# Linformer attention and maxout FFN on one core: softmax sums of a batch in one bank by 128x32 column tiles, spread over partitions by DMA

## The chip, the cores and the metric

The kernel runs on one core of a Trainium2 chip. The metric is device time in microseconds (us). A measured time is some 2 us longer than the span that the profile of the same execution shows (405.52 us against 403.5 us before), so spans are compared with spans and times with times. PE is TensorE, PEld its weight loads, DVE is VectorE, ACT is ScalarE, POOL is GpSimd, SP is SyncE; SPq is SP's sequencer, which here only issues DMAs.

## The reference, cut to what matters

```python
k_proj = einsum('ks,bhsd->bhkd', E, k)            # 1024 keys become 64; v with F likewise
scores = scale * matmul(q, k_proj^T)               # 8 batches, 8 heads, 1024 queries, 64 keys
attn   = exp(scores - max) / (sum(exp) + 1e-9)
x      = matmul(attn, v_proj) -> [8192, 512]       # heads side by side
h      = max(x @ w1, x @ w2, x @ w3)               # 512 -> 768, three times
out    = h @ w_out                                 # 768 -> 512
```

## The kernel before

The FFN runs batch by batch, in two chunks of 512 tokens. A chunk is six `up` steps of 12 matmuls (128x512) and four `down` groups of 6. The attention of batch n is woven into the FFN of batch n-1: a plan says which pieces are put behind which step. The key `(ch, step)` is chunk and step; steps 0 to 5 are `up`, 6 to 9 are `down`. So batch 3's attention stands in the plan of b = 2.

Scores are kept with keys on partitions, so that the sum over keys is a matmul with ones. It gives every sum 64 times, on the very partitions where it is needed:

```python
def pair_mm(b, g, lo, nsi, w):              # one pair of heads: four 64x64 matmuls, side by side
    t, ns = two()                           # two PSUM banks of eight
    p = pTs[b, g, lo]                       # exp(scores)
    for c in range(2):
        rows = slice(c * HALF, (c + 1) * HALF)
        for hp in range(2):
            nc.tensor.matmul(out=t[hp * HALF:(hp + 1) * HALF, c, 0:nsi * HALF],
                             lhsT=w(rows, hp), rhs=p[rows, hp, :], start=True, stop=True)
    ...
def za(b, g, ...):                          # sums, values, inversion, multiply of one pair
    z  = sums(b, g, lo, nsi)                # pair_mm with ones
    av = values(b, g, lo, nsi)              # pair_mm with v_proj
    invert(b, g, lo, nsi, z)                # ACT: Ln, then Exp(-x), each 128x1024
    scale_x(b, g, lo, nsi, av)              # DVE: xT = av * zi, 128x1024
def qd(b):                                  # turn the queries of batch b
    ...                                     # four DVE copies into q_p
    last_T[b] = nc.sync.dma_start_transpose(out=qTs[b]..., in_=q_p...)     # SP's queue
# plan, b == 2                                    # plan, b >= 3 (n = b + 1)
(0, 2): [kproj(3), vproj(3), ld(4)],              (0, 1): [za(n, 0), sc(n, 1)],
(0, 3): [kt(3)],                                  (0, 3): [za(n, 1), sc(n, 2)],
(0, 4): [sc(3, 0)],                               (0, 6): [qd(n + 1)],
(0, 6): [za(3, 0), sc(3, 1)],                     (0, 9): [za(n, 2), sc(n, 3),
(1, 0): [za(3, 1), sc(3, 2), qd(4)],                       kproj(n + 1), vproj(n + 1)],
(1, 2): [za(3, 2), sc(3, 3), kproj(4), ...],      (1, 1): [kt(n + 1), ld(n + 2)],
(1, 4): [kt(4)], (1, 5): [za(3, 3), sc(4, 0)]     (1, 3): [za(n, 3), sc(n + 1, 0)]
```

The transposes, the stores of the output and, after the change, the new DMAs all go through SP, which issues them in the order of the program, each with its wait (the profile after shows a store that was ready at 144.09 us leave at 151.71, behind a transpose).

Names in the profiles: `q_p` and `qT` are the queries before and after the transpose, `pT` is exp(scores), `vp` the projected values, `xT` the attention's output that the up matmuls read, `h1s` a copy of the first up product, `m` and `hT` the two maxima (the down matmuls read `hT`), `zd` and `zi_all` the inverted sums in DRAM and on the partitions. `banks` is PSUM, the eight banks that matmuls write.

The softmax here doesn't subtract the row's maximum and nothing guards it: scores larger than these inputs give would overflow.

## Time and profile before

The median of three runs is 405.52 us (405.26 to 405.64).

| what | where it is read | value |
|---|---|---|
| PE busy | page, part 1 | 98% of a 403.5 us span |
| PE busy in the FFN of batches 3, 4, 5 | stretches | 47.18 of 47.25, 47.00 of 47.00, 47.00 of 47.00 us |
| sums and values of a pair; scores of a pair | chain of waits | 0.56 us; 0.22 us |
| DVE, ACT busy in such a stretch | stretches | 23.94 us each |

The busy time of each engine in stretches that I cut where a batch's last down group ends in the chain (columns: stretch, its length, PE, PEld, DVE, ACT, POOL busy with instruction counts, granted clock as a share of full speed, DMA share, GB/s; the DMA share adds up the packets' times over 16 engines and can pass 1). Here those of the FFN of batches 2 to 5 of the kernel before:

```profile
122.47:172.70 50.23, 49.91 (x313) 23.24 (x312) 25.51 (x40) 25.48 (x37) 5.26 (x6) 1.00 0.93 179
172.70:219.95 47.25, 47.18 (x276) 21.20 (x274) 23.94 (x36) 23.94 (x34) 2.63 (x3) 1.00 0.87 176
219.95:266.95 47.00, 47.00 (x276) 21.22 (x274) 23.94 (x36) 23.94 (x34) 2.63 (x3) 1.00 0.67 134
266.95:313.95 47.00, 47.00 (x275) 21.30 (x274) 23.94 (x36) 23.94 (x34) 0.00 (x0) 1.00 0.22 69
```

PE has no gap there to win back: only work taken off PE can shorten a stretch. The chain of waits (start, length, what) shows what that work costs. L222 is `pair_mm`, L202 the scores, L508 the up matmuls:

```profile
219.95 5.18 PE banks L508 x24
225.13 0.56 PE banks L222 x8
225.69 0.22 PE banks L202 x4
225.91 5.29 PE banks L508 x24
```

Twenty-four up matmuls take 5.18 us, 0.216 us each, and 5.29 after attention work: I put the 0.11 us down to the return to the 128x128 shape. Four 64x64 matmuls side by side take about 0.22 us, and going to that shape takes about 0.12 us more (0.56 - 2 x 0.22).

### The profile page before, as it was taken

How to read it: one execution, taken by the hardware profiler on the slowest of the kernel's cores; microseconds unless marked ns; L12 is line 12 of the kernel's file. 1: busy time of each engine (PE TensorE's matmuls, PEld its weight loads, DVE VectorE, ACT ScalarE, POOL GpSimd, SP SyncE). 2: the span in 40 equal slices, each digit the busy share in tenths (PEclk: the TensorE clock that was granted, in tenths of full speed). 3: DMA queues.
4: the chain of work that ended last, by engine and by line, in shares of the span. 5: the costliest groups of instructions: out<-in, count | busy, mean ns of one | idle time of the engine just before them, and what ended most of it. 6: DMA issues, size and time to landing. Idle time of an engine off the chain costs nothing.

```text
span 403.5 us, 5873 instructions
## 1 busy us (share of the span) xinstructions
PE 394.5 (98%) x2351; PEld 178.5 (44%) x2351; DVE 203.5 (50%) x314; ACT 189.4 (47%) x274; POOL 31.6 (8%) x44
## 2 busy tenths in 40 slices
PE   7899999999999999999999999999999999999996
PEld 3444444344444435444544445444544444444443
DVE  2348755761764527537353655626364363525251
ACT  2622537525672376555643555437535555432322
POOL 7340001001000100200100002000000000000000
PEclk9999999999999999999999999999999999999999
DMA  8999999959907996992799029960510202020202
GB/s 150 207 205 207 231 201 163 246 119 193 219 2 215 190 222 106 137 241 40 210 180 208 30 15 238 201 173 0 137 73 2 104 2 104 0 106 0 106 0 105
DMA packets 62667, 53.33 MB, mean 132 GB/s; under 512 B 30128, under 2 KB 58288, under 8 KB 62640
## 3 DMA queue, kind: packets, MB, share of 16 engines
q0 software_dynamic: 28512, 28.31, 44.1%
q1 hardware_dynamic: 33984, 24.51, 20.6%
q8 instruction: 18, 0.29, 0.3%
q10 hardware_dynamic: 144, 0.13, 0.1%
q14 instruction: 9, 0.07, 0.1%
HBM read 57.15 MB, written 16.78 MB: 183 GB/s over the span
## 4 chain that ended last, share of the span: by engine, by line
PE 82%; DMA 11%; ACT 2%; DVE 1%; POOL 1%; issue 1%; DVEq 0%; ACTq 0%; POOLq 0%
PE banks L508 56%; PE banks L605 18%; DMA v_t<-in_v_dram 7%; PE banks L222 4%; DMA w_sb<-in_moe_w_dram 3%; PE banks L286 3%; PE banks L202 2%; ACT zi L241 1%; DVE xT L252 1%; ACT zl L235 1%; DMA out_dram<-o_sb 0%; POOL k_t L148 0%; POOL q_t L153 0%; POOL v_t L148 0%; DVE m L570 0%
## 5 line engine op out<-in xcount | busy, mean ns | idle before, releaser
L508 PE MATMUL banks<-xT,w_sb 128*128 128x512 bf16 x1152 | 257.9, 379 | 1.5 <-DMA w_sb<-in_moe_w_dram 1.2
L508 PEld LDWEIGHTS <-w_sb 128*128 128x128 bf16 x1152 | 109.5, 98 | 138.1 <-issue 10.6
L570 DVE TENSOR_TENSOR m<-banks,h1s 128x512 f32<-128x512 f32 x90 | 62.1, 690 | 85.0 <-ACT h1s L566 52.1
L566 ACT COPY h1s<-banks 128x512 f32<-128x512 f32 x90 | 52.5, 583 | 90.3 <-PE banks L508 88.2
L605 PE MATMUL banks<-wout_sb,hT 128*128 128x512 bf16 x378 | 85.7, 379 | 0.1
L252 DVE TENSOR_TENSOR xT<-banks,zi 128x1024 bf16<-128x1024 f32 (+1 forms) x36 | 39.8, 1106 | 73.6 <-ACT zi L241 54.2
L518 DVE TENSOR_TENSOR hT<-banks,m 128x512 bf16<-128x512 f32 x90 | 62.3, 692 | 10.0 <-PE banks L508 0.8
L99 ACT COPY o_sb<-banks 128x512 f32<-128x512 f32 (+1 forms) x56 | 32.6, 581 | 52.4 <-PE banks L605 52.4
L605 PEld LDWEIGHTS <-hT 128*128 128x128 bf16 x378 | 36.0, 98 | 45.5 <-issue 3.1
L235 ACT ACTIVATE zl<-banks 128x1024 f32<-128x1024 f32 (+1 forms) x36 | 33.5, 930 | 31.4 <-PE banks L222 30.5
L213 ACT ACTIVATE pT<-banks 128x1024 bf16<-128x1024 f32 (+1 forms) x36 | 33.2, 930 | 15.5 <-PE banks L202 15.5
L241 ACT ACTIVATE zi<-zl 128x1024 f32<-128x1024 f32 (+1 forms) x36 | 34.6, 962 | 1.2
L191 POOL DMA_DIRECT2D q_t<-in_q_dram x7 | 6.2, 880 | 202.4 <-DVE kp L99 80.2
L222 PE MATMUL banks<-pT,ones 64*64 64x512 bf16 (+1 forms) x144 | 13.7, 374 | 0.7 <-DVE xT L252 0.3
L222 PE MATMUL banks<-pT,vp 64*64 64x512 bf16 (+1 forms) x144 | 13.3, 355 | 0.4 <-DVE vp L99 0.4
L202 PE MATMUL banks<-qT,kpT 64*64 64x512 bf16 (+1 forms) x144 | 13.3, 358 | 0.3 <-DVE m L570 0.3
L286 PEld LDWEIGHTS <-efT 128*64 128x64 bf16 x224 | 11.6, 110 | 3.4 <-issue 2.7
L99 DVE CAST vp<-banks 64x256 bf16<-64x256 f32 (+1 forms) x18 | 7.1, 397 | 7.6 <-ACT vp L99 3.7
L222 PEld LDWEIGHTS <-ones 64*64 64x64 bf16 x144 | 4.4, 103 | 14.3 <-issue 14.2
L99 DVE COPY q_p<-q_t 128x1024 bf16<-128x1024 bf16 x28 | 10.0, 420 | 0.0
L99 ACT CAST vp<-banks 64x256 bf16<-64x256 f32 x14 | 5.1, 365 | 8.9 <-PE banks L286 8.7
L99 DVE COPY o_sb<-banks 128x512 f32<-128x512 f32 (+1 forms) x9 | 5.8, 654 | 4.5 <-DMA out_dram<-o_sb 4.5
(51 smaller groups left out, 106.5 us busy)
## 6 DMA issues: line engine op xcount, KB each, us to landing
out_dram<-o_sb SPq DMA_DIRECT2D x30, 512.0 KB, 3.2
q_t<-in_q_dram POOLq DMA_DIRECT2D x7, 1024.0 KB, 9.4
k_t<-in_k_dram POOLq DMA_DIRECT2D x7, 1024.0 KB, 13.6
v_t<-in_v_dram POOLq DMA_DIRECT2D x7, 1024.0 KB, 18.6
w_sb<-in_moe_w_dram POOLq DMA_DIRECT2D x5, 384.0 KB, 12.7
k_t<-in_k_dram POOLq DMA_DIRECT2D x2, 512.0 KB, 8.9
v_t<-in_v_dram POOLq DMA_DIRECT2D x4, 256.0 KB, 12.2
wout_sb<-in_moe_w_out_dram POOLq DMA_DIRECT2D x1, 768.0 KB, 15.7
```

Of the source, the lines that this page charges most:

```text
L99: done = {"v": nc.vector.tensor_copy, "s": nc.scalar.copy, "g": nc.gpsimd.tensor_copy}[eng](out=o, in_=i)
L213: nc.scalar.activation(out=pTs[b, g, lo], in_=t, func=AF.Exp, scale=scale)
L222: nc.tensor.matmul(out=t[hp * HALF:(hp + 1) * HALF, c, 0:nsi * HALF], lhsT=w(rows, hp), rhs=p[rows, hp, :], start=True, stop=True,)
L235: nc.scalar.activation(out=zl, in_=t, func=AF.Ln)
L241: nc.scalar.activation(out=zi, in_=zl, func=AF.Exp, scale=-1.0)
L252: nc.vector.tensor_tensor(out=xTs[b][:, g, lo:lo + nsi, :].rearrange("a (c s) p -> a c (s p)", c=2), in0=t, in1=zi, op=ALU.mult,)
L286: nc.tensor.matmul(out=t[hh * HALF:(hh + 1) * HALF, 0:width], lhsT=efT[:, si, (kv - 1) * KP:kv * KP], rhs=qkv[b][kv][:, heads[hh], si, :], ...
L508: nc.tensor.matmul(out=h, lhsT=w_sb[i][:, ct, jt * P:(jt + 1) * P], rhs=xTs[b][:, ct, ch * SPC:(ch + 1) * SPC, :], start=(ct == first), st ...
L518: nc.vector.tensor_tensor(out=o, in0=h, in1=other, op=ALU.max)
L566: nc.scalar.copy(out=h1s, in_=h[0][0])
L570: nc.vector.tensor_tensor(out=m12, in0=h[1][0], in1=h1s, op=ALU.max)
L605: nc.tensor.matmul(out=o_ps, lhsT=hTs[b, ch][:, jt, tt * P:(tt + 1) * P], rhs=wout_sb[:, jt, :], start=(jt == 0), stop=(jt == NJT - 1),)
```

## The change

The intent: every sum is needed 64 times, but it need be computed only once. `pick` holds, for each head of a pair and each half of the chunk, a block of ones in 8 columns. All 16 rows of sums of a batch come from eight matmuls of 128x32 into one bank; ACT inverts one 128x512 tile instead of four of 128x1024; a small store (32 KB) and four broadcasts (512 KB each) through DRAM put the inverses on the 128 partitions. To give the DMAs time, scores and sums move to the start of the first chunk, and values with their multiplies (`vx`) to the second chunk.

```diff
+            for hp in range(2):
+                for g in range(NPAIR):
+                    nc.tensor.matmul(
+                        out=t[32 * g:32 * (g + 1), :], lhsT=pick[:, hp, :],
+                        rhs=pTs[b, g, 0][:, hp, :], start=(hp == 0), stop=(hp == 1),
+                    )
+            nc.scalar.activation(out=zlc, in_=t, func=AF.Ln)
+            nc.scalar.activation(out=zic, in_=zlc, func=AF.Exp, scale=-1.0)
+            nc.sync.dma_start(out=zd.rearrange("g h c f -> (g h c) f"),
+                              in_=zic.rearrange("(a r) f -> a r f", r=8)[:, 0, :])
+            for u in range(2):
+                gs = slice(2 * u, 2 * u + 2)
+                for hp in range(2):
+                    nc.sync.dma_start(out=zi_all(b)[hp * HALF:(hp + 1) * HALF, gs],
+                                      in_=zd[gs, hp].partition_broadcast(HALF))
 ...  plan, b == 2
+                (0, 0): [kproj(3), vproj(3), ld(4)],
+                (0, 1): [kt(3)],
+                (0, 2): [sc(3, 0, now=True), sc(3, 1)],
+                (0, 4): [sc(3, 2, now=True), sc(3, 3)],
+                (0, 5): [qd(4)],
+                (0, 6): [zc(3)],
+                (1, 2): [kproj(4), vproj(4), ld(5), vx(3, 0), vx(3, 1)],
+                (1, 3): [kt(4)],
+                (1, 5): [vx(3, 2), vx(3, 3), sc(4, 0)],
 ...  plan, b >= 3
+            (0, 1): [sc(n, 1, now=True), sc(n, 2, now=True), sc(n, 3)],
+            (0, 3): [zc(n)],
+            (1, 2): [vx(n, 0), vx(n, 1)],
+            (1, 4): [vx(n, 2), vx(n, 3)],
+            out[0, 2] = [qd(n + 1)]
+            out[1, 2] = [kproj(n + 1), vproj(n + 1)] + out[1, 2]
+            out[1, 3] = [kt(n + 1)]
+            out[1, 4] += [sc(n + 1, 0)]
```

(Cut: the plan's lines that these replace, the loads' places, the tiles, `vx`, six instead of four buffers for exp(scores), one buffer for the inverses of a whole batch.)

More of the change, by code (lines that the diff above doesn't have):

```diff
@@ L52 @@
     att = ctx.enter_context(tc.tile_pool(name="att", bufs=2))
+    scratch = ctx.enter_context(
+        tc.tile_pool(name="scratch", bufs=2, space=bass.MemoryType.DRAM)
+    )
     psum = ctx.enter_context(tc.tile_pool(name="psum", bufs=1, space=bass.MemoryType.PSUM))
@@ L119 @@
     ones = const.tile([P, HALF], BF16, name="ones")
+    pick = const.tile([P, 2, 32], BF16, name="pick")
     warm = const.tile([P, 512], BF16, name="warm")
@@ L174 @@
     nc.vector.memset(ones, 1.0)
+    nc.vector.memset(pick, 0.0)
+    for hp in range(2):
+        for c in range(2):
+            at = hp * 16 + c * 8
+            nc.vector.memset(pick[c * HALF:(c + 1) * HALF, hp, at:at + 8], 1.0)
     load_w(0, slice(0, 2))
@@ L211, in exps @@
         t, ns, ready = sc
-        pTs[b, g, lo] = att.tile([P, 2, CHUNK], BF16, name="pT", bufs=4)[:, :, 0:nsi * HALF]
+        pTs[b, g, lo] = att.tile([P, 2, CHUNK], BF16, name="pT", bufs=6)[:, :, 0:nsi * HALF]
         nc.scalar.activation(out=pTs[b, g, lo], in_=t, func=AF.Exp, scale=scale)
@@ L230, in sums, with zi_all, zc, f @@
         return pair_mm(b, g, lo, nsi, lambda rows, hp: ones[rows])
+    zi_alls = {}
+    def zi_all(b):
+        if b not in zi_alls:
+            zi_alls[b] = att.tile([P, NPAIR, 2, CHUNK], FP32, name="zi_all", bufs=1)
+        return zi_alls[b]
+    def zc(b):
+        def f():
+            t, ns = bank()
+            for hp in range(2):
[3 more added lines that the diff above has]
+                        rhs=pTs[b, g, 0][:, hp, :], start=(hp == 0), stop=(hp == 1),
+                    )
+            ready = pe(2 * MM + 0.1)
+            zlc = att.tile([P, CHUNK], FP32, name="zlc", bufs=1)
+            nc.scalar.activation(out=zlc, in_=t, func=AF.Ln)
+            runs("s", ready, 0.6, ns)
+            zic = att.tile([P, CHUNK], FP32, name="zic", bufs=1)
+            nc.scalar.activation(out=zic, in_=zlc, func=AF.Exp, scale=-1.0)
+            when = runs("s", ready, 0.63) + 9.0
+            zd = scratch.tile([NPAIR, 2, 2, CHUNK], FP32, name="zd")
+            nc.sync.dma_start(
+                out=zd.rearrange("g h c f -> (g h c) f"),
+                in_=zic.rearrange("(a r) f -> a r f", r=8)[:, 0, :],
+            )
+            for u in range(2):
+                gs = slice(2 * u, 2 * u + 2)
+                for hp in range(2):
+                    nc.sync.dma_start(
+                        out=zi_all(b)[hp * HALF:(hp + 1) * HALF, gs],
+                        in_=zd[gs, hp].partition_broadcast(HALF),
+                    )
+            for g in range(NPAIR):
+                zis[b, g, 0] = zi_all(b)[:, g], when
+        return f
+    def vx(b, g):
+        def f():
+            scale_x(b, g, 0, SI, values(b, g, 0, SI))
+        return f
     def invert(b, g, lo, nsi, z):
@@ L237, in invert @@
         if nsi == SI:
-            zi = att.tile([P, 2, CHUNK], FP32, name="zi", bufs=2)
+            zi = zi_all(b)[:, g]
         else:
@@ L263, in run_later, with sc @@
         later.clear()
-    def sc(b, g, lo=0, nsi=SI):
+    def sc(b, g, lo=0, nsi=SI, now=False):
         def f():
             t = scores(b, g, lo, nsi)
-            later.append(lambda: exps(b, g, lo, nsi, t))
+            if now:
+                exps(b, g, lo, nsi, t)
+            else:
+                later.append(lambda: exps(b, g, lo, nsi, t))
         return f
@@ L656, in plan @@
             return {
-                (0, 2): [kproj(3), vproj(3), ld(4)],
-                (0, 3): [kt(3)],
-                (0, 4): [sc(3, 0)],
-                (0, 6): [za(3, 0), sc(3, 1)],
-                (1, 0): [za(3, 1), sc(3, 2), qd(4)],
-                (1, 2): [za(3, 2), sc(3, 3), kproj(4), vproj(4), ld(5)],
-                (1, 4): [kt(4)],
-                (1, 5): [za(3, 3), sc(4, 0)],
+                (0, 0): [kproj(3), vproj(3), ld(4)],
[7 more added lines that the diff above has]
+                (1, 5): [vx(3, 2), vx(3, 3), sc(4, 0)],
             }
@@ L668, in plan @@
         out = {
-            (0, 1): [za(n, 0), sc(n, 1)],
-            (0, 3): [za(n, 1), sc(n, 2)],
-            (0, 9): [za(n, 2), sc(n, 3)],
-            (1, 3): [za(n, 3)],
+            (0, 1): [sc(n, 1, now=True), sc(n, 2, now=True), sc(n, 3)],
+            (0, 3): [zc(n)],
+            (1, 2): [vx(n, 0), vx(n, 1)],
+            (1, 4): [vx(n, 2), vx(n, 3)],
         }
         if n + 1 < B:
-            out[0, 6] = [qd(n + 1)]
-            out[0, 9] += [kproj(n + 1), vproj(n + 1)]
-            out[1, 1] = [kt(n + 1)]
-            out[1, 3] += [sc(n + 1, 0)]
+            out[0, 2] = [qd(n + 1)]
+            out[1, 2] = [kproj(n + 1), vproj(n + 1)] + out[1, 2]
+            out[1, 3] = [kt(n + 1)]
+            out[1, 4] += [sc(n + 1, 0)]
         if n + 2 < B:
-            out[1, 1] += [ld(n + 2)]
+            out[1, 3] += [ld(n + 2)]
         return out
```

## The prediction

> **What bounds the kernel.** TensorE. The page gives PE 98% of a 403.5 us span; the stretch by stretch view gives 47.18 of 47.25 us busy in batch 3's stretch (172.7 to 219.95 us) and 47.00 of 47.00 in batches 4 and 5. The chain of waits after 150 us is almost all matmuls, back to back: 24 up matmuls take 5.18 us, 0.216 us each. ACT and DVE are each about half busy (23.94 of 47.0 us), DMA 0.87, 0.67, 0.22 and 0.12 of the stretches of batches 3 to 6. So only PE work removed, or new PE waits, can move the time.
>
> **Removed and added on PE.** In the chain a pair's sums and values together (8 matmuls, 64x64) take 0.56 us; scores take 0.22, and 0.34 where they stand alone; the up matmuls after them take 5.29 instead of 5.18. I read that as 0.216 us for each group of four concurrent matmuls and 0.11 to 0.12 us for each change of array shape, in and out. The Trainium skill, "TensorEngine Tiling (Array Packing)", Tiling Modes, says that changing the mode drains TensorE, and that 128x32 has four independent tiles; the trace agrees on the first with 0.11 us; no run shows 128x32 yet.
> - Sums before: 4 groups x 0.216 = 0.86 us a batch. After: 8 matmuls in 2 groups of four, 0.43 us if the column tiles run side by side. Saved 0.43.
> - Shape changes: four excursions a batch both before and after, but values now follow the projections directly; about 0.1 us saved.
> Estimate: 0.5 us x 5 batches (3 to 7) = 2.5 us. Nothing else on the critical path becomes shorter.
>
> **Removed elsewhere.** ACT: per batch four Ln of 1.03 us and four Exp of 1.06 us become one of each on 128x512, about 0.6 us: 7 us of ACT a batch. DVE's 1.23 us multiplies stay. Both engines have slack, so this is worth almost nothing directly; value banks are freed sooner.
>
> **Moved and added.** Sums now go through DRAM: one 32 KB store and four 512 KB broadcasts, 2 MB a batch, on SP's queue behind the transpose (3.9 to 7.0 us on SP, 6.8 us to landing). Estimate from the issue table (512 KB stores land in 3.2 us): inverted 1.4 us after the sums, small store landed 4 to 8 us after them, first broadcasts 4 to 6 us later, the last within about 16 us. Use comes about 20 us after the sums in batches 4 to 7: in time. In batch 3 the gap is only about 14 us, with the transpose and loads around it (DMA 0.93 busy in batch 2's stretch): DVE may wait 0 to 3 us there and hold up the maxima behind it. Three scores in a row take six PSUM banks and queue ACT's copies behind exponentials: 0 to 0.3 us a batch.
>
> **Prediction.** 405.5 - 2.5 + 0.5 = 403.5 us; range 401.6 to 406.5. Chances: faster by over 2% 0.02, within 2% 0.92, slower by over 2% 0.06.
>
> **What would show it.** New sums: eight matmuls in 0.43 to 0.5 us, plus about 0.23 for shape changes. Batch stretches of 47.0 become about 46.5. ACT busy falls by about 35 us. DVE multiplies wait for no DMA, except perhaps in batch 3. PE stays at 98%.
>
> **What would make it wrong.** The column tiles run one after another (1.7 us a batch: 6 us back, no gain). The broadcasts, 64 partitions reading the same few KB of DRAM, run far slower than stores, so that DVE blocks, PSUM fills and PE waits in every batch. SP, blocked on the small store, delays output stores until output buffers run out.

## More of the kernel before

What SP does matters later. Its timeline before has each transpose in a time of its own; the lines are start, length, engine, operation, and the count:

```profile
154.41 4.72 SPq L333 DMA_TRANSPOSE qT<-q_p  x1
171.06 2.63 SPq L619 DMA_DIRECT2D out_dram<-o_sb  x2
192.15 3.97 SPq L333 DMA_TRANSPOSE qT<-q_p  x1
```

## The result, and the profile after

| | median of 4 runs | range |
|---|---|---|
| before | 405.58 us | 405.26 to 405.74 |
| changed | 410.85 us | 410.17 to 412.47 |

The ratio is 1.0137 (95% interval 1.0104 to 1.0170): 1.4% slower. Ratios here and below are the mean time of one kernel's fast runs over that of the other's fast runs of the same rounds, so they are not quite the ratio of the medians that I quote. The output is correct.

Part 1 of the page after:

```profile
PE 389.1 (95%) x2269; PEld 177.1 (43%) x2311; DVE 202.4 (50%) x319; ACT 156.1 (38%) x244; POOL 31.4 (8%) x44
```

PE is at 95% instead of 98%: it waits now. ACT's busy time fell from 189.4 to 156.1 us, as intended. The same stretches of the changed kernel, the FFN of batches 2 to 5:

```profile
121.99:178.37 56.38, 50.35 (x300) 23.07 (x304) 25.31 (x40) 19.08 (x31) 5.26 (x6) 0.97 1.07 212
178.37:225.30 46.93, 46.19 (x263) 21.06 (x266) 23.65 (x36) 17.24 (x28) 2.62 (x3) 1.00 0.92 196
225.30:272.22 46.92, 46.18 (x262) 21.03 (x266) 23.65 (x36) 17.23 (x28) 2.62 (x3) 1.00 0.84 183
272.22:319.15 46.93, 46.19 (x263) 21.00 (x266) 23.66 (x36) 17.23 (x28) 0.00 (x0) 1.00 0.46 120
```

One stretch holds the loss: batch 2's, which carries batch 3's attention, went from 50.23 to 56.38 us, and its granted clock from 1.00 to 0.97. The others became 0.07 to 0.32 us shorter, where I had expected about 0.5. (Some matmul records are missing from this trace, 2269 of 2311, so its PE busy times are a little low; the lengths of the stretches don't depend on that.) Stretch by stretch the 5.0 us between the two spans are: start -0.48, batch 2 +6.15, batches 3 to 6 -0.32, -0.08, -0.07, -0.15, the rest -0.05.

The chain of waits inside batch 2's stretch, after:

```profile
151.71 2.06 DMA zd<-zic
...
154.50 9.54 DMA zi_all<-zd
...
164.16 1.24 DVE xT L308
...
165.44 6.88 PE banks L567 x24
```

The store of the inverses starts at 151.71, the broadcasts hold up everything until 164.04, then DVE multiplies and PE goes on. And the next 24 up matmuls (L567, before L508) take 6.88 us instead of 5.18. The timeline around it shows who held whom (the bracket gives the idle time before and what ended it):

```profile
142.16 0.61 PE L256 MATMUL banks<-pT,pick 128*32 128x512 bf16 x8
143.08 8.54 SPq L392 DMA_TRANSPOSE qT<-q_p  x1
143.46 0.63 ACT L265 ACTIVATE zic<-zlc 128x512 f32<-128x512 f32 x1
151.71 0.55 SPq L268 DMA_DIRECT2D zd<-zic  x1
153.79 3.19 SPq L275 DMA_DIRECT2D zi_all<-zd  x4
154.16 0.88 POOL L200 DMA_DIRECT2D q_t<-in_q_dram  x1 [21.51 <-DMA qT<-q_p]
164.16 2.36 DVE L308 TENSOR_TENSOR xT<-banks,zi_all 128x1024 bf16<-128x1024 f32 x2 [6.07 <-DMA zi_all<-zd]
165.44 6.88 PE L567 MATMUL banks<-xT,w_sb 128*128 128x512 bf16 x24 [5.66 <-DVE xT L308]
```

The inverses are ready at 144.09 (143.46 + 0.63), but SP is busy with batch 4's transpose until 151.6, so the store leaves 7.6 us late. The broadcasts then take until 164. DVE, which wanted them at 158.1, waits 6.07 us; the multiplies hold PSUM banks, and PE waits 5.66 us.

In the other batches there is a small wait in a different place. The timeline of batch 4's stretch, near the end of its last up step:

```profile
263.84 2.76 PE L567 MATMUL banks<-xT,w_sb 128*128 128x512 bf16 x12
264.15 2.35 DVE L308 TENSOR_TENSOR xT<-banks,zi_all 128x1024 bf16<-128x1024 f32 x2
264.92 0.58 ACT L625 COPY h1s<-banks 128x512 f32<-128x512 f32 x1 [2.84 <-PE banks L567]
265.40 1.03 ACT L222 ACTIVATE pT<-banks 128x1024 bf16<-128x1024 f32 x1
266.42 0.68 DVE L629 TENSOR_TENSOR m<-banks,h1s 128x512 f32<-128x512 f32 x1
267.20 0.69 DVE L577 TENSOR_TENSOR hT<-banks,m 128x512 bf16<-128x512 f32 x1
267.95 4.28 PE L664 MATMUL banks<-wout_sb,hT 128*128 128x512 bf16 x19 [0.26 <-DVE hT L577]
```

The up step ends on PE at 266.4. Five down matmuls can follow, until 267.5; the sixth needs the last `hT`, which DVE finishes at 267.9. PE stands about 0.4 us. The two multiplies stand in front of the last two maxima on DVE, but an exponential on ACT ends at about the same time, so the trace alone leaves two suspects.

### The profile page after: what moved, and what is told of

Read it like the earlier page. It is cut to its first block, busy times and chain, and to the rows that moved or that the text cites. A ratio compares the mean times of both kernels' runs of the same rounds, so it can differ in the third digit from the quotient of the medians.

```text
span 408.5 us, 5754 instructions
## 1 busy us (share of the span) xinstructions
PE 389.1 (95%) x2269; PEld 177.1 (43%) x2311; DVE 202.4 (50%) x319; ACT 156.1 (38%) x244; POOL 31.4 (8%) x44
## 4 chain that ended last, share of the span: by engine, by line
PE 83%; DMA 6%; DVE 4%; ACT 2%; issue 2%; POOL 1%; SPq 0%; DVEq 0%; ACTq 0%; POOLq 0%
PE banks L567 56%; PE banks L664 18%; DMA w_sb<-in_moe_w_dram 3%; PE banks L345 3%; DMA zi_all<-zd 2%; DVE xT L308 2%; PE banks L231 2%; PE banks L211 2%; ACT zl L291 1%; ACT zi_all L297 1%; DVE hT L577 1%; DVE m L629 1%; PE banks L256 1%; ACT pT L222 1%; DMA zd<-zic 1%
## 5 line engine op out<-in xcount | busy, mean ns | idle before, releaser
L567 PE MATMUL banks<-xT,w_sb 128*128 128x512 bf16 x1120 | 256.1, 381 | 9.9 <-DVE xT L308 5.8
L567 PEld LDWEIGHTS <-w_sb 128*128 128x128 bf16 x1152 | 109.9, 98 | 145.4 <-issue 18.7
L664 PEld LDWEIGHTS <-hT 128*128 128x128 bf16 x378 | 35.7, 98 | 47.1 <-DVE hT L577 4.5
L308 DVE TENSOR_TENSOR xT<-banks,zi_all 128x1024 bf16<-128x1024 f32 x28 | 33.3, 1219 | 23.2 <-ACT zi_all L297 17.0
L291 ACT ACTIVATE zl<-banks 128x512 f32<-128x512 f32 (+1 forms) x16 | 13.0, 810 | 9.8 <-PE banks L231 8.9
L102 DVE CAST vp<-banks 64x256 bf16<-64x256 f32 (+1 forms) x18 | 7.1, 397 | 11.2 <-ACT vp L102 7.8
L231 PE MATMUL banks<-pT,vp 64*64 64x512 bf16 (+1 forms) x144 | 11.8, 362 | 0.4 <-DVE vp L102 0.4
L211 PE MATMUL banks<-qT,kpT 64*64 64x512 bf16 (+1 forms) x144 | 11.5, 361 | 0.0
L297 ACT ACTIVATE zi_all<-zl 128x1024 f32<-128x1024 f32 x8 | 8.5, 1057 | 0.3
L200 POOL DMA_DIRECT2D k_t<-in_k_dram x7 | 6.1, 876 | 26.2 <-PE banks L345 25.9
L345 PE MATMUL banks<-k_t,efT 128*64 128x256 bf16 x112 | 7.5, 276 | 0.0
```

What stands on the lines that cost most here:

```text
L102: done = {"v": nc.vector.tensor_copy, "s": nc.scalar.copy, "g": nc.gpsimd.tensor_copy}[eng](out=o, in_=i)
L211: nc.tensor.matmul(out=t[c * HALF:(c + 1) * HALF, hp, 0:n * P], lhsT=kpTs[b][rows, g, :], rhs=qTs[b][rows, at:at + n, :], start=True, stop ...
L291: nc.scalar.activation(out=zl, in_=t, func=AF.Ln)
L308: nc.vector.tensor_tensor(out=xTs[b][:, g, lo:lo + nsi, :].rearrange("a (c s) p -> a c (s p)", c=2), in0=t, in1=zi, op=ALU.mult,)
L345: nc.tensor.matmul(out=t[hh * HALF:(hh + 1) * HALF, 0:width], lhsT=efT[:, si, (kv - 1) * KP:kv * KP], rhs=qkv[b][kv][:, heads[hh], si, :], ...
L567: nc.tensor.matmul(out=h, lhsT=w_sb[i][:, ct, jt * P:(jt + 1) * P], rhs=xTs[b][:, ct, ch * SPC:(ch + 1) * SPC, :], start=(ct == first), st ...
```

## The experiments

The theory after these readings: (1) the sums themselves save what they should; (2) nearly all of the loss is batch 3's store, queued on SP behind a transpose; (3) the slow matmuls after the wait are a cold clock; (4) 0.4 us a batch is given back at the last `hT` because of DVE. Rivals: broadcasts out of a few KB of DRAM are slow whenever they run; the slow matmuls are contention; ACT, not DVE, delays the last `hT`. Eleven kernels were run, all correct. "Stretch" is always batch 2's unless another is named.

### e1: the transpose after the broadcasts

```diff
-                (0, 5): [qd(4)],
                 (0, 6): [zc(3)],
+                (0, 7): [qd(4)],
```

> The changed kernel with one step moved: in the plan of batch 2, batch 4's DMA transpose is asked for after batch 3's small store and broadcasts instead of ahead of them. Theory A (queue order): the changed kernel loses its time in one place, where SP issues the transpose for 8.54 us (143.08 to 151.7) while the inverted sums have been ready since 144.1, so the broadcasts land 6 us too late and PE waits 5.7 us and then runs slow. With the order turned the store lands near 146, the first broadcasts near 156, before DVE wants them at 158; the PE wait in batch 2's stretch is gone, the stretch falls from 56.4 to about 49 us and the time from 410.9 to 403 to 404 us. Rival B (slow broadcasts): four 512 KB broadcasts out of the same few KB of DRAM beside the loads need over 10 us whenever they start, and the transpose beside them makes them slower still; then DVE still waits several us and the time stays above 408 us.

Measured: 405.37 us (404.59 to 405.76), ratio 0.9992 (0.9979 to 1.0005). The stretch is 49.97 us instead of 56.38. SP's timeline:

```profile
145.99 0.53 SPq L268 DMA_DIRECT2D zd<-zic  x1
150.56 2.60 SPq L275 DMA_DIRECT2D zi_all<-zd  x4
154.01 12.08 SPq L392 DMA_TRANSPOSE qT<-q_p  x1
184.74 9.41 SPq L392 DMA_TRANSPOSE qT<-q_p  x1
```

The store leaves as soon as the inverses are there, and DVE waits for no broadcast. So the order on SP is the cause of the large wait: only the transpose, with its DVE copies, was moved. (Batch 5's loads wait for that transpose and so move too, from 154.2 to 168.6 us; e10 measures what they cost.) The rival falls for batch 3. The time is 1.4 to 2.4 us above what I expected of it, and part of that is a new wait: the transpose, now behind the broadcasts, lands 14.1 us after its issue, and the scores of batch 4 wait 0.75 us for it. This run's start was also slow: batch 2's stretch begins at 123.86 us here, at 121.99 in the changed kernel.

The last line above is batch 5's transpose. It stands at the same place of the plan in both kernels, but here batch 5's loads are still running beside it (they land at 193.0 us). In the changed kernel they had landed at 186.3 us, and SP's timeline there has:

```profile
189.28 4.82 SPq L392 DMA_TRANSPOSE qT<-q_p  x1
```

So beside loads a transpose held SP for 9.41 us, without them for 4.82. Broadcasts ahead of it do the same: with half of their bytes (e8 against e7) batch 4's transpose held SP for 7.99 us instead of 12.30.

### e2: PE fed while it waits

```diff
+            if b == 4:          # in kt(b), where PE stops; bank ns[1] is held there and unused
+                for _ in range(26):
+                    nc.tensor.matmul(out=psum_t[:, ns[1], :], lhsT=warm[:, 0:P], rhs=warm, start=True, stop=True)
```

(Cut: the line that tells the kernel's own planner of them.)

> The changed kernel with 26 dummy matmuls (26 x 0.216 = 5.6 us, zeros, into the second, unused bank that the transposes of batch 4's key projection already hold) put where PE waits 5.7 us in batch 3's stretch. DVE's wait for the broadcasts and the release at about 164 us stay. Theory A (cold clock): the first 8 or so up matmuls after the wait took 0.43 us instead of 0.216 because PE had idled; with PE fed they take 0.216, and the time falls by 1.7 us, to about 409.1 us. Rival B (contention with the DMA traffic that lands in that moment, or a late release): those matmuls stay slow and the time stays at 410.9 us, or grows if the dummies overrun the wait.

Measured: 410.70 us (409.20 to 411.81), ratio 1.0124 (1.0104 to 1.0143). In the profiled run, the one of 409.20 us, DVE still waits 5.9 us for the broadcasts, but the timeline of PE goes on at full rate:

```profile
160.21 5.78 PE L417 MATMUL banks<-warm 128*128 128x512 bf16 x26
164.58 2.36 DVE L308 TENSOR_TENSOR xT<-banks,zi_all 128x1024 bf16<-128x1024 f32 x2 [5.88 <-DMA zi_all<-zd]
165.86 5.34 PE L571 MATMUL banks<-xT,w_sb 128*128 128x512 bf16 x24
```

Twenty-four matmuls in 5.34 us against 6.88 (busy times on the timeline, the last end modelled), beside the same DMA traffic (282 GB/s over them here, 287 in the changed kernel): contention falls as the reason, the idle time is it. The granted clock says so too: in the changed kernel it is 0.50 from 165.17 to 168.58 us (stretches view), here it stays at 1.00. The Trainium skill says the same in "TensorE: Matmul & The Clock Gate", Part 1: the array falls to half its clock after at least one idle window of about 3.4 us. The traces agree: after the wait of 5.66 us the next eight starts were 0.32 to 0.43 us apart, and so were eight after 4.8 us (e6) and 3.5 us (e10, there from the fifth on), nine after 6.45 us (e3) and twelve after 5.4 us (e11); after 2.0 us (e4) none were. The gain in time is not confirmed by the medians: 410.70 against 410.85. Two of the four runs had a mean granted clock of 0.995 as in the changed kernel, which suggests that 26 matmuls did not cover the wait there; the other two (0.999 and 1.000) took 409.20 and 410.47. The expected 1.7 us are seen in the profiled run alone (stretch 54.66 us instead of 56.38).

### e3: the second chunk's attention one step earlier

```diff
-            (1, 2): [vx(n, 0), vx(n, 1)],
-            (1, 4): [vx(n, 2), vx(n, 3)],
+            (1, 1): [vx(n, 0), vx(n, 1)],
+            (1, 3): [vx(n, 2), vx(n, 3)],
 ...  projections (1, 2) -> (1, 1), key transposes and loads (1, 3) -> (1, 2), next scores (1, 4) -> (1, 3)
```

> The changed kernel with the second chunk's attention work of batches 4 to 7 one FFN step earlier (projections and the first two value pairs after up step 1, key transposes after 2, the last two value pairs and the next scores after 3 instead of 4); batch 3's plan and its late broadcasts stay. Theory A: in the stretches of batches 4 to 7 the change does save about 0.46 us of PE work a batch, but 0.4 us of it goes back where the down matmuls wait for the last hT, because two 1.2 us multiplies sit before the last maxima on DVE; with a step between them the wait is gone, the stretches fall from 46.92 to about 46.5 us, the time by 4 x 0.4 = 1.6 us to about 409.2 us. Rival B: the wait for hT comes from something else (ACT's copies behind the exponential of the next scores), or the broadcasts are not there one step earlier: stretches stay at 46.9 us or grow.

Measured: 410.11 us (408.38 to 411.41), ratio 1.0111 (1.0093 to 1.0129). The stretches of batches 3 and 4 (batch 5's is 46.49 us too):

```profile
180.29:226.78 46.49, 46.49 (x267) 21.13 (x266) 23.67 (x36) 17.25 (x28) 2.63 (x3) 1.00 0.89 192
226.78:273.27 46.49, 46.49 (x267) 21.13 (x266) 23.67 (x36) 17.26 (x28) 2.62 (x3) 1.00 0.86 189
```

46.49 us and PE busy throughout: the wait for the last `hT` is gone and the full saving, 47.00 - 46.49 = 0.51 us, is there. The median fell by only 0.7 us. In the profiled run (410.61 us) batch 2's stretch was 1.1 us longer than in the changed kernel (wait 6.45 us instead of 5.66, and 7.22 us instead of 6.88 for the slow matmuls) and began 0.8 us later, which ate the gain; the other runs have no profile.

### e4: both moves

The diffs of e1 and e3 together.

> Both moves together (transpose after the broadcasts in batch 2's plan, attention work of batches 4 to 7 one step earlier in the second chunk). If the two losses are separate, they add: 410.9 - 7.4 - 1.6 = about 402 us, 0.9% below the kernel before, which is the 2.5 us that were predicted for the PE work, plus the half of a us that the new plan of batch 2 saves. If the first move only shifts the wait (rival B of the first run), over 406 us.

Measured: 405.70 us (404.76 to 406.88), ratio 1.0001 (0.9985 to 1.0016): 3.7 us more than expected. The two gains are there (stretch 50.32 us, batches 4 and 5 at 46.49), but the early multiplies of batch 4 now wait for their own broadcasts, and PE with them for 2.0 us, and the wait for the transpose grew to 1.1 us. In e3 batch 4 had been in time: batch 5's transpose, which stands ahead of batch 4's store on SP, held SP for 4.82 us there, after batch 5's loads. Here those loads start 12.8 us later (167.8 us instead of 155.0), the transpose runs beside them and holds SP for 9.43 us. A wait taken away had hidden another.

### e5: batch 3 the old way

The plan of b = 2 is that of the kernel before; all else as in the changed kernel.

> One part of the change undone: batch 3 gets its sums the old way (batch 2's plan is that of the kernel before), batches 4 to 7 keep the new way as in the changed kernel. Theory A: the whole loss is batch 3's late broadcasts, so it goes: no PE wait over 1 us in batch 2's stretch, which takes about 50.2 us again; batches 4 to 7 gain about 0.1 us each over the kernel before, as in the changed kernel, where the wait for the last hT gives the rest back. Time about 405.2 us, the same as before within 0.2%. Rival B: the broadcasts of batches 4 to 7 also cost, hidden so far because the late batch 3 had let the loads run ahead; then batch 4 is late here and the time is 407 us or more.

Measured: 404.43 us (404.21 to 406.48), ratio 0.9986 (0.9963 to 1.0009). The stretch is 50.24 us, PE waits for no broadcast. This undoes the loss from the other side. The rival (the later batches cost too) falls.

### e6: half of the bytes

```diff
-            zic = att.tile([P, CHUNK], FP32, name="zic", bufs=1)
+            zic = att.tile([P, CHUNK], BF16, name="zic", bufs=1)      # zd and zi_all likewise
```

> The changed kernel with the inverted sums kept in bf16 (store 16 KB, broadcasts 256 KB, so half of the bytes; order of the queue as in the changed kernel). It tells apart the two parts of the delay: 7.6 us behind the transpose on SP, and about 10 us from issue to landing of the first broadcasts. Theory A (bytes count): the store still goes out near 151.7, the first two broadcasts land about 5 us after issue, near 159, DVE waits about 1 us instead of 6, PE under 1 us, the clock stays up: 404 to 405 us. Rival B (the landing time is a fixed cost or is set by the loads beside it): the broadcasts still need 8 us or more, PE waits 3 us or more, the time stays over 408 us. The result is a little less exact and should still be correct.

Measured: 410.48 us (410.03 to 413.17), ratio 1.0132 (1.0104 to 1.0160). My theory of this run was wrong. From the chain:

```profile
153.10 2.10 DMA zd<-zic
...
155.93 8.51 DMA zi_all<-zd
```

The broadcasts of half the size still take 8.51 us instead of 9.54, and PE waits 4.8 us. In the 40 us from 140 to 180 the loads held 80% of the engines (queue view). So bytes alone don't mend a late start.

### e10: the loads held back

```diff
+            if i == 0 and b == 5:
+                after(dma, mark[3, 1])       # batch 5's loads wait for DVE's second multiply of batch 3
 ...  plan, b == 2
-                (1, 2): [kproj(4), vproj(4), ld(5), vx(3, 0), vx(3, 1)],
+                (1, 2): [kproj(4), vproj(4), vx(3, 0), vx(3, 1), ld(5)],
```

> The changed kernel with batch 5's three 1 MB loads held until DVE has made batch 3's second multiply (a dependency is added; in the changed kernel they start at 154 to 158 us, together with the broadcasts of 153.8 to 157). Order of the queue and bytes stay as in the changed kernel, so the broadcasts still start 7.6 us late. Theory A (contention with the loads makes the broadcasts slow; halving their bytes in e6 didn't help because the loads held 80% of the engines): the first two broadcasts land 5 to 6 us after issue instead of 9.5, near 159.5, DVE waits about 1.5 us instead of 6.1, PE under 1 us, no cold stretch: about 404.5 us. Rival B (64 rows reading the same few KB of DRAM are slow by themselves): the landing stays near 9.5 us, the PE wait near 5.7 us, the time near 410.5 us.

Measured: 408.62 us (408.21 to 409.25), ratio 1.0078 (1.0062 to 1.0093). The chain:

```profile
151.56 2.07 DMA zd<-zic
...
154.35 7.42 DMA zi_all<-zd
```

The loads, which in the changed kernel start in the same moment, cost the broadcasts 2.1 us (9.54 to 7.42); I had expected about 4. DVE waits 3.9 us and PE 3.5, still enough to cool the clock. So of DVE's wait of 6.1 us about 2.1 are contention with batch 5's loads. What remains when they are held, 3.9 us, I put down to the late start; no run has the early store beside the early loads. Each of e6 and e10 alone leaves a wait; the order of the queue (e1) removes all of it, because it also lets the broadcasts run before those loads begin.

### e11: only the next scores later

```diff
-            out[1, 4] += [sc(n + 1, 0)]
+            out[1, 6] = [sc(n + 1, 0)]
```

> The changed kernel with only the next batch's first scores moved, from after up step 4 to after the first down group, in batches 4 to 7; the two multiplies stay where they were. It tells apart what e3 moved together. Theory A (DVE's two 1.2 us multiplies ahead of the last maxima delay the last hT): PE still starts the last down matmuls of the first group 0.4 us late in batches 3 to 6, and the extra change of shape adds about 0.2 us: stretches about 47.1 us, time about 411 us. Rival B (ACT's exponential of the next scores delays the copy that the last maxima need): the wait is gone, stretches about 46.7 us, time about 410 us.

Measured: 412.53 us (411.85 to 412.94), ratio 1.0167 (1.0154 to 1.0181). The stretches are 47.37 us, and the timeline shows the wait again, with no exponential near it:

```profile
265.23 2.34 DVE L308 TENSOR_TENSOR xT<-banks,zi_all 128x1024 bf16<-128x1024 f32 x2
265.78 0.59 ACT L625 COPY h1s<-banks 128x512 f32<-128x512 f32 x1 [2.62 <-PE banks L567]
267.49 0.68 DVE L629 TENSOR_TENSOR m<-banks,h1s 128x512 f32<-128x512 f32 x1
269.03 0.39 PE L664 MATMUL banks<-wout_sb,hT 128*128 128x512 bf16 x1 [0.48 <-DVE hT L577]
```

ACT's copy is done at 266.4, and DVE begins the maximum at 267.5, when its two multiplies are over. The rival (ACT) falls; DVE's order is the cause. The stretches are longer than the 47.1 us that I expected, with the change of shape counted in, because the scores (0.22 us) had filled a part of the wait: without them PE reaches it earlier and waits 0.48 us instead of 0.26. The slow matmuls after batch 3's wait took 0.8 us more as well (7.72 us instead of 6.88).

### e7, e8, e9: nothing given back

e7 is e4 with the transpose after the sums in batches 4 to 7 too:

```diff
-            out[0, 2] = [qd(n + 1)]
+            out[0, 4] = [qd(n + 1)]
```

> Both moves of the fourth run, and the same order of the queue in every batch: the next batch's DMA transpose is asked for one step after the sums, not one step before them, in batches 4 to 7 too. The fourth run waited 2.0 us in batch 3's stretch for the broadcasts of batch 4 and 1.1 us for the transpose behind batch 3's broadcasts. Theory A: with the store no longer behind the transpose, the first wait goes (the store leaves 2 us earlier or more), the second stays: about 403.6 us. Rival B: the broadcasts of batch 4 are late because of the loads beside them, whatever the order on SP; then a wait of 1 us or more stays and the time is 405 us or more.

Measured: 403.14 us (402.56 to 403.77), ratio 0.9936 (0.9924 to 0.9949). The wait for batch 4's broadcasts is gone; only the wait for the transpose in batch 2's stretch stays, 1.0 us.

e8 is e7 with the inverses in bf16.

> As e7, with the inverted sums in bf16, so 1 MB instead of 2 MB of broadcasts a batch. If contention of broadcasts, loads and the transpose is what is left, the wait for the transpose (0.75 to 1.1 us) and what remains of the wait for batch 4's broadcasts go as well: 402.5 to 403 us, 0.7% below the kernel before: 5 x 0.46 us of PE work and nothing given back. If 403.6 us or more stays, the rest lies elsewhere.

Measured: 401.37 us (401.31 to 401.54), ratio 0.9895 (0.9881 to 0.9908), 1.1% below the kernel before, and still correct. PE waits for nothing after 100 us, and the broadcasts of batch 3 land in 4.6 us (median) where those of e7 needed 7.5. Two stretches, of batches 2 and 3:

```profile
122.09:171.11 49.02, 49.02 (x305) 22.69 (x304) 25.22 (x40) 19.08 (x31) 5.26 (x6) 1.00 1.01 195
171.11:217.62 46.51, 46.51 (x267) 21.04 (x266) 23.66 (x36) 17.24 (x28) 2.63 (x3) 1.00 1.05 212
```

Halving the bytes gained nothing clear of noise in e6 (410.48 against 410.85 us), where the late start came first, and 1.8 us here.

e9 has batch 3 the old way and batches 4 to 7 as in e7.

> Batch 3 the old way (batch 2's plan is that of the kernel before), batches 4 to 7 the new way with the two mended places of e7 (a step earlier in the second chunk, transpose after the sums). It measures what the sums change alone is worth where nothing is given back. Theory A: batch 2's stretch about 50.2 us as before, the stretches of batches 3 to 6 46.5 instead of 47.0 us: 405.6 - 4 x 0.5 = 403.6 us, or up to 1 us less, since the fifth run's median was already 1.2 us below the kernel before. If 405 us or more comes out, the predicted 0.46 us a batch is not there even without waits.

Measured: 403.26 us (402.85 to 404.74), ratio 0.9940 (0.9927 to 0.9952). The stretches of batches 3 to 5 are 46.51 to 46.52 us. Four batches with the new sums and no new waits are worth 2.4 us.

## Why the prediction was wrong

The prediction was 403.5 us (401.6 to 406.5); 410.85 came out, outside the range, with the sign wrong.

- **What bounds the kernel: right.** PE, and only its work or its waits moved the time.
- **The work taken off PE: right.** I put it at 0.5 us a batch; e3 measured 0.51 (47.00 to 46.49 us). The eight 128x32 matmuls run four side by side: in the chain they take 0.55 us with the change of shape in, and each four start within 0.01 us. The Trainium skill's "TensorEngine Tiling (Array Packing)", Available Configurations, gives four tiles for 128x32, and the trace agrees. ACT fell by 33 us where I had said about 35.
- **The step that failed: "In batch 3 ... DVE may wait 0 to 3 us there and hold up the maxima behind it", entered in the sum with 0.5 us for all waits together.** The mechanism was named, its size was not. I let the store land 4 to 8 us after the sums, with the transpose at the 3.9 to 7.0 us that it took on SP before. It landed 11.0 us after them (142.8 to 153.8): the transpose held SP for 8.54 us. (In e1, with no transpose ahead of it, it landed 5.9 us after them, as I had said.) The transpose had been moved from 154.4 us, after batch 4's loads had drained (DMA share 0.41 from 148 to 152 us, none from 152 to 154), to 143.1 us, into those loads (share 1.24 to 1.26). That the loads stretch it is what batch 5's transpose shows (9.41 us beside loads, 4.82 without, see e1). I gave the first broadcasts 4 to 6 us; they took 10.3 us from there, of which e10 puts 2.1 us on batch 5's loads, set off by the same late transpose. Use came about 15.3 us after the sums, close to the 14 that I had said. So DVE waited 6.07 us and PE 5.66 us.
- **A term that I left out: the clock.** After the wait of 5.66 us PE ran at half rate for some matmuls (granted clock 0.50 for 3.41 us): 24 took 6.88 us instead of 5.18, 1.7 us more.
- **A second term that I left out: the last `hT`.** I looked for small waits at the scores (0 to 0.3 us a batch) and found none worth naming. The 0.4 us a batch were at the end of the last up step, where the moved multiplies stand in front of the last maxima on DVE (e3, e11). This ate most of the saving in batches 4 to 6: 0.07 to 0.15 us was left of about 0.5.

For batch 2's stretch the sum is: 5.66 + 1.70 - 6.15 = 1.21 us, which is what its PE work and its old small wait must have given; e8, with no waits, shows the same: 50.23 - 49.02 = 1.21. What stays open: why the start of the kernel, up to batch 2, varies by up to 2 us between runs whose code there is the same (in the two slowest, e1 and e9, the granted clock is 0.50 for 3.4 us near 10 us, but e6 starts late without that), and how much of the clock's 1.7 us the unprofiled runs lost.

## What to carry to other kernels

When a result is sent through DMA so that a bound engine has less to do, cost the queue that issues the DMA: list what stands ahead of it there and what each of those takes in the new place, not in the old one. Here the transpose ahead of a short store cost 7.6 us, and the store itself took 2.1. Then look at what the released work stands in front of on the engines with slack, and count a long wait of PE with the slow clock behind it: here waits of 3.5 us and more had it, one of 2.0 us had not.

## What the Trainium skill lacked or had wrong

- "DMA: Bandwidth & Descriptors": how long a DMA transpose holds the engine that issues it stands there only in a table on another chip, for earlier generations and without the data transfer; I found no time for it beside other traffic. Here one transpose of a batch's queries held SP for 3.95 to 8.64 us (before, changed, e6), where a plain DMA took it 0.3 to 1.2 us, for 9.41 us beside loads (e1) and for up to 12.3 us behind 2 MB of broadcasts (e7).
- The same page: I found no figure for broadcasts out of a few KB of DRAM. Here, of four of 512 KB to 64 partitions each, the quickest landed in 5.0 to 5.1 us and the slowest in 10.8 to 11.2 us with no loads beside them (batches 6 and 7 of the changed kernel), and in up to 14.3 us with loads (batch 4). Of 256 KB each they landed in 3.5 to 5.3 us (e8).
- "TensorEngine Tiling (Array Packing)", Key Properties, says that a change of mode drains the array and gives no cost: 0.11 to 0.12 us each way here, for 64x64 and for 128x32 alike (0.55 - 2 x 0.216 us in, 5.29 - 5.18 out).
